# Spectral filter and gated feed-forward on one core: order of the inverse column transforms, number of half-blocks, places of folds, add-backs and loads

## The chip, the core and the metric

The kernel runs on one core of one Trainium2 chip. The metric is the device time of the whole program in microseconds (us). The median of three runs before the change is 499.27 us (499.16 to 499.53). TensorE multiplies matrices, VectorE (DVE) and ScalarE (ACT) work element by element and empty TensorE's accumulators (PSUM), GpSimd (POOL) does a few small operations, and SyncE (SP) issues nearly all DMAs.

## The reference

Two layers work on `x` of 2048 rows and 576 columns in bfloat16. The first is a global filter: layer norm, a real two-dimensional Fourier transform, a multiplication by a complex weight, the inverse transform, and the addition of `x`. The second is a feed-forward layer with a gate of width 4608.

```python
def _A_ref(x, w_r, w_i):
    X = rfft2(x.astype(float32), axes=(-2, -1))
    X = X * (w_r + 1j * w_i)
    return irfft2(X, s=(S, D), axes=(-2, -1)).astype(bfloat16)

def _B_ref(x, w_gate, w_up, w_down):
    return (gelu(x @ w_gate) * (x @ w_up)) @ w_down

h  = x + _A_ref(layernorm(x), w_r, w_i)
h2 = h + _B_ref(layernorm(h), w_gate, w_up, w_down)
```

## The kernel before, in words

All engines run instructions in the order in which the kernel's text issues them; that order is written out by hand. The 2048 rows lie as 16 tiles of 128 (`h_sb[:, h, :]`, `h` from 0 to 15). All transforms are matrix products on TensorE. PSUM is used as four rotating slots of two banks (`two`), so every use waits until the use four places before it has been emptied.

**Spectral part.** After the row transforms the work goes over nine "channels" `k` in the order 1, 2, ..., 7, 0 (0 carries 8 along). Per step of the loop at lines 668 to 706: `f2` and `f3` do forward products on TensorE, ScalarE copies their results, `wmul` on VectorE multiplies by the weights and writes a tile `Zt`, and `i3` does the inverse products of a channel from its `Zt` and the table `TI`. ScalarE (for one part VectorE) copies the results of `i3` into one of two collecting tiles: `EO[0]` takes channels 1 to 4, `EO[1]` takes 0 and 5 to 7. `inv_cols(x, g)` (line 632) then transforms the columns of pair `g` of row tiles (0 to 7) out of `EO[x]`: ten matmuls with weights of 58 rows into `cs_ps`, followed by an eviction with scaling into `cs` (pairs 0 and 1) or `cw`/`cwb` (pairs 2 to 7). `inv_cols(0, ...)` needs channels 1 to 4 alone; `inv_cols(1, ...)` needs all. Lines 707 to 715 set the order behind the loop: three transforms of `EO[0]`, channel 7's `i3`, four transforms, channel 0's `i3`, one transform. In the last step of the loop channel 6's `i3` stands ahead of all of them.

**Putting rows together.** `add_rows(g)` (line 757) multiplies pair `g` by the matrix `G16` into two PSUM slots `y_ps`, and the result is added to `h_sb`. For pairs 0 and 1 that is done at once. For pairs 2 to 7 it is spread over the feed-forward blocks in three steps: `fold` (line 745; four VectorE operations of 288 elements into `both`), `add_both` (line 780, the "add-back": eight matmuls and two VectorE additions), and `stats2` per row tile (line 785). After these, `norm2` (line 789) writes the normalised rows and `flip` (line 802) sends them by a transposing DMA, issued by SP, into `hl`, the matrix `Bt` read by the gate products. Row tiles 0 and 1 are transposed on TensorE instead; 2 and 3 go through `flip` during the first half-blocks.

**Feed-forward part.** Four chunks of 512 rows. For each chunk, 36 blocks of 128 gate and up columns (`gate`, line 889: 18 matmuls with 64-row weights, Gelu on ScalarE into `g_sb`, a multiplication on VectorE into `P_sb`, which frees the PSUM slot), then four down products (`acc`, line 938). Weights come in groups of three blocks (`load_gu`). The first chunk is split: `NH` half-blocks work on columns 0 to 255 (row tiles 0 and 1), before tiles 2 and 3 have arrived. The main loop then starts at its block 0; its blocks below `NH` work on columns 256 to 511 alone, and from block `NH` on they work on all 512.

`todo` is a table from the number of the block (0 to 143) to the small steps issued right behind that block; `after` is the same for the half-blocks. SP issues `flip`, `load_gu` and the loads of the down weights in the order of the text, and each of them waits at the head of SP's queue. `load_wd2` loads the last third of the down weights, `wd_2`, in six slices of two blocks each (288 KB); slice `i` holds blocks 24 + 2i and 25 + 2i.

Of the kernel before, what the change touches and what calls it, by code (L numbers as in the profile page):

```python
# [41 lines left out]
def kernel_body(  # L42
# [23 lines left out]
    def two(name):  # L66
        return psum.tile([P, 2, 512], FP32, name=name, tag="two", bufs=4)
# [72 lines left out]
    def load_gu(g, t=None):  # L140
        gc = slice(g % (NFT // FQ) * FQ * P, (g % (NFT // FQ) + 1) * FQ * P)
        if t is None:
            t = wgpool.tile([P, NR, FQ * P], BF16, name="wgu", tag="wgu")[:]
        for c, w in ((0, B_w_gate), (1, B_w_up)):
            nc.sync.dma_start(t[64 * c : 64 * c + 64], w[:, gc].rearrange("(r k) c -> k r c", k=64))
        return t
# [11 lines left out]
    NWA = 12  # L158
# [90 lines left out]
    def angle_c(sl):  # L249
        drop_sign(ab[:, sl], ab[:, sl])  # L250
# [4 lines left out]
    def cosine(sl):  # L255
        A.activation(TF[:, sl, 1, :], ab[:, sl], ACT.Sin, bias=nhpib[:], scale=2.0 * PI / S)

    def minus_sine(sl):
        V.tensor_scalar(TF[:, sl, 0, :], TF[:, sl, 2, :], -1.0, None, op0=ALU.mult)

    def turn_tf(sl):
        nc.sync.dma_start(
            TI[:, sl].rearrange("p k r q -> p (k r) q"), TF[:, sl].rearrange("p k r q -> p (k r q)"), transpose=True
        )
# [207 lines left out]
    def f2(c):  # L472
        ps = two("pq_ps")
        col = slice(slot[c] * P, (slot[c] + 1) * P)
        steps = [(par, t) for par in range(2) for t in (par, par + 2, 4)]
        if c == order[0]:
            steps.sort(key=lambda s: s[1] == 4)
        for par, t in steps:
            T.matmul(  # L479
                ps[:, par, 0:JP],  # L480
                lhsT=Bt[:, t, col],
                rhs=DT[:, t // 2, par] if t < 4 else DF[:, par],
                start=(t == par),
                stop=(t == 4),
            )
        pq[c] = wk.tile([P, 2, JP], BF16, name="pq", tag="pq", bufs=6)
        pq_ps[c] = ps

    def f2_out(c, copy=A.copy, rs=slice(0, 2)):
        copy(  # L490
            pq[c][:, rs].rearrange("p r (j a) -> p r j a", a=2),
            pq_ps[c][:, :, 0:JP].rearrange("p a (r j) -> p r j a", r=2)[:, rs],
        )
# [5 lines left out]
    def f3(k, half):  # L499
        ps = two("gh_ps")  # L500
        if k == 0:
            p0, p8 = pq[0], pq[8]
            t0, t1 = (NS, C) if half else (C, SN)
            for b, kk, p in ((0, 0, p0), (1, 8, p8)):
                comb(ps[:, b, 0:J], kk, t0, p[:, 0, 0:J], t1, p[:, 1, 0:J])
            if half == 0:
                xab[k] = wk.tile([P, 2, 2, JP], BF16, name="xab", tag="xab", bufs=2)
            A.copy(xab[k][:, half, :, 0:J], ps[:, :, 0:J])
            return
        p, q = pq[k], pq[k + 8]  # L510
        gh = wk.tile([P, 2, JP], BF16, name="hs" if half else "g", tag="hs" if half else "g", bufs=2)
        r = half
        comb(ps[:, r, 0:J], k, C, p[:, r, 0:J], SN, q[:, r, 0:J])
        comb(ps[:, 1 - r, 0:J], k, C, q[:, r, 0:J], NS, p[:, r, 0:J])
        if k == order[0] and half:
            hk[k] = ps
            return
        A.copy(gh[:, :, 0:J], ps[:, :, 0:J])
        if half == 0:
            gk[k] = gh  # L520
            return
        hk[k] = gh

    def sum_of(k, half):
        g, hs = gk[k], hk[k]
        if half == 0:
            xab[k] = wk.tile([P, 2, 2, JP], BF16, name="xab", tag="xab", bufs=2)
        x = xab[k]
        V.tensor_tensor(  # L529
            x[:, 1, ::-1, 0:J] if half else x[:, 0, :, 0:J],  # L530
            g[:, :, 0:J],
            hs[:, :, 0:J],
            ALU.add if half else ALU.subtract,
        )
# [97 lines left out]
    def inv_cols(x, g):  # L632

        ps = two("cs_ps")
        for w in range(NW):
            for e in range(2):
                rows = slice(64 * e, 64 * e + JW)
                T.matmul(  # L638
                    ps[:, e, 0:JP],
                    lhsT=EO[x][rows, w, 2 * g : 2 * g + 2].rearrange("p h e k l -> p (h e k l)"),  # L640
                    rhs=DQ[rows, w] if w or e else DT[rows, 0, :, 0, :],
                    start=(w == 0),
                    stop=(w == NW - 1),
                )
        pv = ps[:, :, 0:JP].rearrange("p t (q a) -> p t q a", q=2)
        if g >= 2:
            if x == 0 or g == 2:
                cw[x, g] = eop.tile([P, 2, JP], FP32, name=f"cw{x}{g}")[:]
            else:
                cw[x, g] = cwb[:, g - 3]  # L650
            dst = cw[x, g].rearrange("p t (a q) -> p t q a", q=2)
            if x == 0 and g == 6:
                V.tensor_scalar(dst, pv, Y_SCALE, None, op0=ALU.mult)
            else:
                A.activation(dst, pv, ACT.Copy, scale=Y_SCALE)
            return
        ts = eop.tile([P, 2, JP], BF16, name=f"cs{x}{g}")
        dst = ts[:].rearrange("p t (a q) -> p t q a", q=2)
        if x == 1 and g == 1:
            V.tensor_scalar(dst, pv, Y_SCALE, None, op0=ALU.mult)  # L660
        else:
            A.activation(dst, pv, ACT.Copy, scale=Y_SCALE)
        cs[x, g] = ts
# [4 lines left out]
    for i in range(n + 1):  # L668
        last = i >= n
        if not last:  # L670
            f2(order[i])
            if i != 1:
                f2_out(order[i])
        if i == 0:
            f2(order[0] + 8)
            angle_c(rest)
            cosine(rest)
            for r in range(2):
                f2_out(order[0] + 8, V.tensor_copy, slice(r, r + 1))
            minus_sine(rest)  # L680

        if 1 <= i <= n:
            f3(order[i - 1], 0)
            f3(order[i - 1], 1)
            if i == 1:
                f2_out(order[1])
                sum_of(order[0], 0)
                sum_of(order[0], 1)
            else:
                if i == 2:  # L690
                    turn_tf(rest)
                    pre = [load_gu(g) for g in range(3)]
                    nc.sync.dma_start(wd_a[:], wd_view[:, 0:NWA, :])
                wmul(order[i - 2], i - 1, order[i - 1])
        if not last and i:
            f2(order[i] + 8)
            f2_out(order[i] + 8)
        if i >= 3:
            for s in range(3):
                i3(order[i - 3], s)  # L700
        if last:
            wmul(order[i - 1], i)
        if i == 1:
            scr_pool.__exit__(None, None, None)
            eop = ctx.enter_context(tc.tile_pool(name="eop", bufs=1, side="right"))
            EO = [eop.tile([P, 5, H, 2, 4, 8], BF16, name=f"EO{x}", tag=f"EO{x}") for x in range(2)]
    for g in (0, 1, 2):
        inv_cols(0, g)
    for s in range(3):
        i3(order[6], s)  # L710
    for g in (3, 4, 5, 6):
        inv_cols(0, g)
    for s in range(3):
        i3(order[7], s)
# [157 lines left out]
    todo = {}  # L872
    for h in range(4, H):
        b = 6 * (h // 2 - 2)
        if h % 2 == 0:
            todo.setdefault((1, 6, 10, 13, 16, 19)[h // 2 - 2], []).append((fold, h // 2))
            todo.setdefault(b + 4, []).append((add_both, h // 2))
        todo.setdefault(b + 5 + h % 2, []).append((stats2, h))
        b = h // 4 * NFT - NFT + 3 * (h % 4) + 2 + 12 * (h < 8)
        todo.setdefault(b, []).append((norm2, h))  # L880
        todo.setdefault(b + 1, []).append((flip, h))

    for i in range(0, NWA, 2):
        todo.setdefault(16 + 3 * i // 2, []).append((load_wd2, slice(i, i + 2)))
    blk = 0
    groups = pre
    NG = NFT // FQ
# [15 lines left out]
        A.activation(g_sb, gu[:, 0, 0:n], ACT.Gelu_apprx_tanh)  # L903
        V.tensor_tensor(p_sb(f)[:, lo:hi], g_sb, gu[:, 1, 0:n], ALU.mult)  # L904

    NH = 11
    after = {
        0: [(sum_squares, 3), (norm2, 2), (flip, 2)],
        1: [(head_rstd, 3)],
# [1 line left out]
    }  # L911
    for f in range(NH):
        gate(0, f, groups[f // FQ], f % FQ, 0, 2 * P)
        for fn, h in after.get(f, ()):
            fn(h)
    for tcnk in range(4):
        for gi in range(NG):
            for i in range(FQ):
                f = gi * FQ + i
                gate(tcnk, f, groups[0], i, 2 * P if tcnk == 0 and f < NH else 0, 4 * P)  # L920
                for fn, h in todo.pop(blk, ()):
# [8 lines left out]
        for st in range(4):  # L930
            h = tcnk * 4 + st
# [85 lines left out]
```

## Time and profile before

| | |
|---|---|
| median of three runs | 499.27 us |
| profiled execution, whole | 499.36 us |
| its span | 497.6 us |
| TensorE busy | 487.6 us |
| VectorE busy | 224.5 us |
| ScalarE busy | 161.6 us |
| gate and up products, `gu` (line 895), share of the chain that ended last | 55% |
| down products, `acc` (line 938), share of that chain | 27% |
| column transforms, `cs_ps` (line 638), share of that chain | 2% |

The profile shows one execution, with all times from the start of its span. "PE" is TensorE's matmuls, "PEld" its weight loads, "SPq" SP's queue of DMA issues. A line of the time line has the start, the length, the engine, the line of the kernel, the operation, the tile written and those read, the shape, and the number merged; the idle time of the engine before it, with what ended it, stands in brackets. The chain lists start, length and work of what ended last. A table by stretches has, for each engine, the busy time and the number of instructions, then the granted clock, the busy share of the 16 DMA engines (over 1 where packets overlap) and GB/s. A matmul's shown length includes the time until its result is there, so starts of neighbours, not lengths, give the pace.

### The profile page before, as it was taken

To read this page: it belongs to the slowest core of one execution; us is meant where nothing else is said; L and a number is where in the kernel's file an instruction comes from. 1 tells how busy PE (TensorE), PEld (TensorE's weight loads), DVE (VectorE), ACT (ScalarE), POOL (GpSimd) and SP (SyncE) were. 2 spreads that over 40 slices of the span, in tenths; PEclk is the share of its full clock that TensorE was granted. 3 is DMA by queue.
4 is the path that set the end of the run, shared out by engine and by line. 5 is a ranking of instruction groups with operands and counts; after the bars stand their busy time and mean duration, and the time that the engine had idled before them with its cause. 6 is when DMAs were issued, how large, how long until landed. Compare 5 with 4: busy or idle time off the path is not lost.

```text
span 497.6 us, 12727 instructions
## 1 busy us (share of the span) xinstructions
PE 487.6 (98%) x5698; PEld 340.2 (68%) x5698; DVE 224.5 (45%) x442; ACT 161.6 (32%) x288; POOL 28.9 (6%) x78
## 2 busy tenths in 40 slices
PE   6999899999999999999999999999999999999997
PEld 2578689888879964444499844444799644445995
DVE  8999786988541244433311244333221333333111
ACT  8999873222211013233200132323110223233000
POOL 8500010201100000000000000000000000000000
PEclk9999999999999999999999999999999999999999
DMA  8739779959990019987730079987700287870000
GB/s 277 229 38 208 198 146 226 177 109 208 212 204 10 3 50 208 204 159 155 155 75 3 1 149 213 187 158 153 144 1 3 75 156 157 158 150 1 13 14 24
DMA packets 89549, 62.33 MB, mean 125 GB/s; under 512 B 23190, under 2 KB 88086, under 8 KB 89494
## 3 DMA queue, kind: packets, MB, share of 16 engines
q1 hardware_dynamic: 89206, 60.34, 60.9%
q0 software_dynamic: 288, 1.18, 0.8%
q8 instruction: 44, 0.72, 0.6%
q14 instruction: 11, 0.09, 0.1%
HBM read 52.65 MB, written 2.36 MB: 111 GB/s over the span
## 4 chain that ended last, share of the span: by engine, by line
PE 88%; DVE 7%; DMA 2%; SPq 1%; ACT 1%; issue 0%
PE gu L895 55%; PE acc L938 27%; PE cs_ps L638 2%; PE acc L957 2%; DVE m L547 2%; DMA h_sb<-in_A_x_dram 1%; PE y_ps L767 1%; SPq L421 1%; DVE xab L529 1%; DVE xn L136 1%; DVE st L117 1%; DVE st L116 1%; DVE Zt L567 0%; PE eo_ps L587 0%; ACT Bt L322 0%
## 5 line engine op out<-in xcount | busy, mean ns | idle before, releaser
L895 PE MATMUL gu<-Bt,wgu 64*128 64x512 bf16 (+1 forms) x2646 | 271.8, 363 | 0.0
L895 PEld LDWEIGHTS <-wgu 64*128 64x128 bf16 x2646 | 144.8, 94 | 123.6 <-DMA wgu<-in_B_w_up_dram 0.4
L904 DVE TENSOR_TENSOR P_sb<-g_sb,gu 128x512 bf16<-128x512 f32 (+1 forms) x155 | 99.9, 647 | 142.6 <-ACT g_sb L903 142.6
L903 ACT ACTIVATE g_sb<-gu 128x512 f32<-128x512 f32 (+1 forms) x155 | 87.8, 567 | 194.8 <-PE gu L895 194.0
L938 PEld LDWEIGHTS <-P_sb 64*128 64x128 bf16 x2160 | 132.7, 94 | 0.6
L938 PE MATMUL acc<-wd,P_sb 64*128 64x288 bf16 x1440 | 93.8, 283 | 0.0
L947 DVE TENSOR_TENSOR part<-part,acc 128x576 f32<-128x576 f32 x15 | 11.3, 754 | 111.3 <-ACT part L946 111.3
L938 PE MATMUL acc<-wd_a,P_sb 64*128 64x288 bf16 x720 | 49.7, 283 | 0.0
L946 ACT COPY part<-acc 128x576 f32<-128x576 f32 x15 | 9.6, 639 | 122.4 <-PE acc L938 122.4
L895 PE MATMUL gu<-Bt,wgu_e 64*128 64x256 bf16 (+1 forms) x144 | 12.5, 322 | 0.0
L792 DVE TENSOR_SCALAR hrow<-h_sb,mv,rstd 128x1152 bf16<-128x1152 bf16 x14 | 12.1, 868 | 0.6 <-POOL rstd L830 0.6
L479 PE MATMUL pq_ps<-DT,Bt 128*128 128x290 bf16 x64 | 12.3, 286 | 0.0
L949 DVE TENSOR_TENSOR h_sb<-h_sb,part 128x576 bf16<-128x576 bf16 x15 | 11.4, 758 | 0.5
L133 POOL TENSOR_TENSOR rstd<-rstd,mhalf 128x1 f32<-128x1 f32 (+1 forms) x16 | 11.4, 713 | 1.3
L895 PEld LDWEIGHTS <-wgu_e 64*128 64x128 bf16 x144 | 10.5, 94 | 1.3
L286 PE MATMUL f2t<-h_sb,ident 128*128 128x512 bf16 x27 | 7.8, 444 | 3.6 <-DMA h_sb<-in_A_x_dram 3.6
L479 PEld LDWEIGHTS <-Bt 128*128 128x128 bf16 x96 | 9.2, 97 | 2.5
L638 PE MATMUL cs_ps<-DQ,EO 58*128 58x290 bf16 x144 | 10.6, 283 | 0.0
L298 PE MATMUL f2t<-F,xn 128*128 128x256 bf16 x64 | 9.3, 275 | 1.4 <-DVE xn L136 1.4
L587 PE MATMUL eo_ps<-TI,Zt 128*128 128x256 bf16 x70 | 8.8, 273 | 1.3 <-DVE Zt L568 1.3
L490 ACT CAST pq<-pq_ps 128x580 bf16<-128x580 f32 x15 | 9.9, 663 | 0.2
L123 ACT ACTIVATE junk<-h_sb 128x576 bf16<-128x576 bf16 x14 | 9.4, 678 | 0.4 <-DMA h_sb<-in_A_x_dram 0.4
(138 smaller groups left out, 276.0 us busy)
## 6 DMA issues: line engine op xcount, KB each, us to landing
wgu<-in_B_w_gate_dram SPq DMA_DIRECT2D x46, 432.0 KB
wgu<-in_B_w_up_dram SPq DMA_DIRECT2D x46, 432.0 KB
wd_a<-in_B_w_down_dram SPq DMA_DIRECT2D x1, 1728.0 KB
wd<-in_B_w_down_dram SPq DMA_DIRECT2D x1, 1728.0 KB
wd<-in_B_w_down_dram SPq DMA_DIRECT2D x6, 288.0 KB
out_dram<-h_sb SPq DMA_DIRECT2D x3, 576.0 KB
h_sb<-in_A_x_dram SPq DMA_DIRECT2D x4, 288.0 KB
h_sb<-in_A_x_dram SPq DMA_DIRECT2D x2, 576.0 KB
```

What stands on the lines that cost most here:

```text
L133: G.tensor_tensor(dst[:, sl], dst[:, sl], mhalf[:, sl], ALU.pow)
L479: T.matmul(ps[:, par, 0:JP], lhsT=Bt[:, t, col], rhs=DT[:, t // 2, par] if t < 4 else DF[:, par], start=(t == par), stop=(t == 4),)
L547: V.tensor_tensor(m[:, :, :, js], x[:, :, :, js], w[:, sl, js].unsqueeze(1).to_broadcast([P, 2, 2, n]), ALU.mult)
L638: T.matmul(ps[:, e, 0:JP], lhsT=EO[x][rows, w, 2 * g : 2 * g + 2].rearrange("p h e k l -> p (h e k l)"), rhs=DQ[rows, w] if w or e else DT ...
L792: V.tensor_scalar(hrow[:], h_sb[:, h, :].rearrange("p (r k) -> p r k", k=64).unsqueeze(2).to_broadcast([P, NR, 2, 64]), mv2[:, h, 0:1], rs ...
L895: T.matmul(gu[:, c, 0:n], lhsT=w[rows, r, i * P : (i + 1) * P], rhs=hl[tcnk % 2][rows, r, lo:hi], start=(r == 0), stop=(r == NR - 1),)
L903: A.activation(g_sb, gu[:, 0, 0:n], ACT.Gelu_apprx_tanh)
L904: V.tensor_tensor(p_sb(f)[:, lo:hi], g_sb, gu[:, 1, 0:n], ALU.mult)
L938: T.matmul(accs[i][:, c, 0:DH], lhsT=p_sb(f)[rows, st * P : (st + 1) * P], rhs=wd[f // NWA][rows, f % NWA, c * DH : (c + 1) * DH], start=( ...
L947: V.tensor_tensor(part, part, accs[1][:, :, 0:DH], ALU.add)
L949: V.tensor_tensor(hv, hv, part, ALU.add)
L957: T.matmul(acc[:, 0, 0:DH], lhsT=p_sb(f)[:, st * P : (st + 1) * P], rhs=wd[f // NWA][:, f % NWA, cc], start=(f == 0), stop=(f == NFT - 1),)
```

## The change

Four edits, in program order. First, `inv_cols(0, 0)` and `inv_cols(0, 1)` are issued inside the last step of the loop ahead of channel 6's `i3`. Behind the loop there are then three transforms (2, 3, 4), channel 7's `i3`, two (5, 6), channel 0's `i3`, and the last one, as before. Second, `NH` is 10 instead of 11. Third, the folds move from behind blocks 1, 6, 10, 13, 16, 19 to 4, 8, 11, 14, 17, 20; the add-backs from 4, 10, 16, 22, 28, 34 to 6, 12, 18, 24, 30, 36; the statistics go two blocks later with them. `norm2` and `flip` keep their places. Fourth, the six slices of `wd_2` are issued behind blocks 17, 21, 25, 29, 33, 35 instead of 16, 19, 22, 25, 28, 31.

```diff
         if not last and i:
             f2(order[i] + 8)
             f2_out(order[i] + 8)
+        if last:
+            inv_cols(0, 0)
+            inv_cols(0, 1)
         if i >= 3:
             for s in range(3):
                 i3(order[i - 3], s)
...
-    for g in (0, 1, 2):
+    for g in (2, 3, 4):
         inv_cols(0, g)
     for s in range(3):
         i3(order[6], s)
-    for g in (3, 4, 5, 6):
+    for g in (5, 6):
         inv_cols(0, g)
     for s in range(3):
         i3(order[7], s)
...
     for h in range(4, H):
         b = 6 * (h // 2 - 2)
         if h % 2 == 0:
-            todo.setdefault((1, 6, 10, 13, 16, 19)[h // 2 - 2], []).append((fold, h // 2))
-            todo.setdefault(b + 4, []).append((add_both, h // 2))
-        todo.setdefault(b + 5 + h % 2, []).append((stats2, h))
+            todo.setdefault((4, 8, 11, 14, 17, 20)[h // 2 - 2], []).append((fold, h // 2))
+            todo.setdefault(b + 6, []).append((add_both, h // 2))
+        todo.setdefault(b + 7 + h % 2, []).append((stats2, h))
...
-    for i in range(0, NWA, 2):
-        todo.setdefault(16 + 3 * i // 2, []).append((load_wd2, slice(i, i + 2)))
+    for i, bk in enumerate((17, 21, 25, 29, 33, 35)):
+        todo.setdefault(bk, []).append((load_wd2, slice(2 * i, 2 * i + 2)))
...
-    NH = 11
+    NH = 10
```

## The prediction

> **What bounds the kernel now.** I read the busy shares first, then the chain that ended last, then TensorE's waits, then the time line around each place that the edits touch.
>
> ```profile
> PE 487.6 (98%) x5698; PEld 340.2 (68%) x5698; DVE 224.5 (45%) x442; ACT 161.6 (32%) x288; POOL 28.9 (6%) x78
> PE 88%; DVE 7%; DMA 2%; SPq 1%; ACT 1%; issue 0%
> ...
> 69.47 15.73 PE gu L895 x288
> ...
> 104.89 11.66 PE gu L895 x108
> ```
>
> TensorE is 98% busy, so only its gaps and its overheads can be won. The two chain rows give the prices of its work: 288 matmuls are 16 half-blocks, 0.983 us each; 108 are 6 full blocks, 1.943 us each. The waits show few gaps behind the first 51 us:
>
> ```profile
> PE eo_ps L587 <- DVE Zt L568: 1.3, 1, 1.3
> PE y_ps L767 <- DVE P_sb L904: 0.2, 1, 0.2
> ```
>
> The time line of TensorE shows where they lie (start, length, what; in brackets the idle time):
>
> ```profile
> 50.43 0.29 PE L497 MATMUL gh_ps<-pq,TF 128*128 128x289 bf16 x1
> 51.98 1.27 PE L587 MATMUL eo_ps<-TI,Zt 128*128 128x256 bf16 x10 [1.26 <-DVE Zt L568]
> 53.17 0.29 PE L638 MATMUL cs_ps<-DT,EO 58*128 58x290 bf16 x1
> ...
> 58.95 1.31 PE L611 MATMUL eo_ps<-TI,Zt 128*64 128x128 bf16 x40
> ...
> 80.01 1.36 PE L895 MATMUL gu<-Bt,wgu 64*128 64x256 bf16 x21
> ...
> 91.77 0.98 PE L767 MATMUL y_ps<-both,G 64*128 64x288 bf16 x8 [0.19 <-DVE P_sb L904]
> 92.48 1.24 PE L895 MATMUL gu<-Bt,wgu_e 64*128 64x512 bf16 x9
> ```
>
> At 51.98 channel 6's products wait for its `Zt`, which VectorE finishes at 51.92; VectorE has no gap from 31 us on, so nothing brings that time forward. 80.01 is block 0 of the main loop, the first work on columns 256 to 511, and it did not wait. The last two rows are the second add-back, late.
>
> **Step 1, the transforms ahead of channel 6.** One column transform takes 0.62 us (53.17, 53.81, 54.43 start its neighbours); two take 1.24. The last matmul before the gap starts at 50.43 and needs 289 columns at the rate of the stream, 0.12 us, so TensorE is free at about 50.55. The trace shows 0.09 us more at each change between full-height and 64-row matmuls (start to start 0.21 us at 52.97 to 53.17, against 0.11 within a run). The two transforms then run 50.64 to 51.88, and with the change back TensorE is ready at 51.97: the gap is filled to the last tenth, and channel 6 still starts at 51.98. Behind it the sequence is three transforms, channel 7, two, channel 0. Channel 7 starts at 55.15 as before (its `Zt` is written at 55.08). Channel 0 started at 58.95 and now starts 1.24 earlier, 57.71; its `Zt`, last written by the operation at 56.90 for 0.46, is there at 57.36. Cover for the added evictions: ScalarE idled 1.14 us from 51.92 (its row at 53.06), and two evictions at 0.67 each end at 53.26, so channel 6's copy slips 0.2. Four rotating PSUM slots carry all of this. The tightest reuse is the third moved-up transform, at 54.46 in the slot of channel 6's copy, free at about 54.3: 0.13 us to spare. Everything behind follows TensorE in relative time. **-1.24 us**; bounds -1.24 and 0 (if slots come free late).
>
> **Step 2, ten half-blocks instead of eleven.** Two halves become one full block: 2 x 0.983 - 1.943 = **-0.02**. But the main loop now begins one half-block sooner after the work before it: 80.01 - 0.98 = 79.03 on the old time line. Its first weights wait for the flips of rows 2 and 3 (DMA transposes issued by SP). The share and GB/s of the DMA engines, last two columns, show them:
>
> ```profile
> 73.04 1.33 SPq L804 DMA_TRANSPOSE Bt<-hrow  x1
> 75.23 1.62 SPq L804 DMA_TRANSPOSE Bt<-hrow  x1
> 74.00:75.50 1.50, 1.50 (x32) 1.38 (x28) 1.23 (x4) 0.48 (x2) 0.29 (x1) 1.00 1.92 171
> 75.50:77.00 1.50, 1.50 (x32) 1.38 (x30) 0.94 (x4) 0.67 (x2) 0.00 (x0) 1.00 0.37 7
> 77.70:78.50 0.80, 0.80 (x20) 0.73 (x18) 0.42 (x1) 0.20 (x2) 0.00 (x0) 1.00 1.57 24
> 78.50:79.10 0.60, 0.60 (x16) 0.56 (x12) 0.33 (x1) 0.23 (x1) 0.00 (x0) 1.00 1.13 253
> 104.00:105.57 1.57, 1.57 (x21) 1.40 (x19) 0.50 (x1) 0.60 (x1) 0.00 (x0) 1.00 1.05 199
> ```
>
> They move bytes until 79.10, with two stretches of almost none; the completion increments of the second come at 79.63 to 79.78. Before, that was 0.23 us early; now it is 0.75 late. The flips' own start hangs on TensorE's earlier work by way of VectorE and POOL, so the 1.24 shifts both alike. **+0.75 us**; bounds 0 and +1.0.
>
> The fourth flip, alone, moved its bytes in 1.57 us (last row) and completed 3.3 us after its issue at 102.81. At that pace the second one would be there at 75.23 + 3.3 = 78.5, before 79.03, and the term would be 0.
>
> The Trainium skill ("DMA: Bandwidth & Descriptors", "Latency and other measured facts") gives DMA transposes 261 GB/s, and its section "Anatomy of one DMA" a fixed cost of about 2.0 us for a DMA issued by GpSimd. My estimate from that page is 2.0 + 295 KB / 261 GB/s = 3.1 us, so no wait here, and a sum lower by 0.75. The lone flip agrees; these two took 5.8 and 4.6 us, and the measurement decides.
>
> **Step 3, folds and add-backs.** Removed: the stall at 91.77. Half-block 10 freed TensorE at 91.41, the eight add-back matmuls take 0.48 undisturbed, and the next block began at 92.48: 0.58 us lost, because fold 3 and two sets of statistics held up the VectorE operations (0.33 each) that free PSUM. **-0.58**. The new schedule puts add-back 2 two half-blocks behind its fold, where three lay between. VectorE's rows after block 1, placed after block 4 (B = end of its matmuls):
>
> ```profile
> 82.70 0.42 DVE L904 TENSOR_TENSOR P_sb<-g_sb,gu 128x256 bf16<-128x256 f32 x1 [0.56 <-ACT g_sb L903]
> 83.03 0.45 DVE L753 TENSOR_TENSOR both<-cw 128x288 bf16<-128x288 f32 x1
> ...
> 84.14 0.45 DVE L754 TENSOR_TENSOR both<-cw 128x288 bf16<-128x288 f32 x1
> 84.51 0.42 DVE L904 TENSOR_TENSOR P_sb<-g_sb,gu 128x256 bf16<-128x256 f32 x1
> ```
>
> Block 1 ended at 80.01 + 2 x 0.983 = 81.98, so the fold's last output is ready at B + 2.16 + 0.45 + 0.05 = 2.66. The add-back's last pair wants it at B + 1.97 + 0.36 = 2.33: +0.33. Half-block 7 then wants the slot of half-block 5, freed at B + 2.53 + 0.41 + 0.05 = 2.99, where TensorE is ready at 2.78: +0.21. Add-back 3, at block 12, has fold 3 (block 8) long behind it. At block 17 row 5's normalisation (0.79) and fold 6 (1.48) lie in front of block 18's multiply: its slot is free at B + 0.93 + 0.60 + 0.79 + 1.48 + 0.69 + 0.05 = 4.54, block 20 wants it at 2 x 1.943 + 0.48 = 4.37: +0.16. The other folds have blocks of 1.943 with 0.61 of VectorE work in them. **+0.70**; bounds 0 and +1.0. Add-back 7 goes to block 36, behind the down products; their slots are emptied under block 36, and nothing waits.
>
> **Step 4, the loads of `wd_2`.** On SP's queue five of six move behind flips and weight loads; the last two go behind the load for group 13. Between 112 and 144 us the DMA engines run without a break at about 210 GB/s, first come first served. The load for group 11, issued at 125.88, came at 137.0 and cost 0.10 us; with one slice (295 KB, 1.4 us) less ahead of it that goes: **-0.10**. The last slices trade places with the load that completed at 148.5, so they come by 148.5; the first down product starts at 143.12, takes 8.82, and reads them from 143.12 + 8.82 x 32/36 = 150.96. 2.5 us to spare: 0.
>
> **Sum.** -1.24 - 0.02 + 0.75 - 0.58 + 0.70 - 0.10 = -0.49. The profiled execution took 499.36 (span 497.6 and 1.76 around it), 0.09 above the median of 499.27. 499.36 - 0.49 = 498.87, as a median 498.8.
>
> **Rivals.** *The flips come in time* (30%). For it: the lone flip's row; the stall between 75.5 and 77.0 has no cause in the edit, and may not recur. Against: the same two flips, the same instructions around them. Sum without the 0.75: 498.0, faster.
> *The last `wd_2` slices are late* (7%): the down product waits at 150.96 for a load issued only after block 33. It turns the sign when the lateness eats the 2.5 us, the 0.5 gained and 1.0 more, so at 4 us later than first come first served makes them, about 152.5; then 500.3 or more. Against: the DMA engines' rate falls to 143 GB/s in 144 to 152, so the queue is running empty there.
> *The transforms do not fill the gap* (5%): their slots or evictions come late, step 1 is worth 0, and the rest adds up to +0.75: 500.0 as a median, within 0.2%.
>
> **How the numbers follow.** A run of this kernel can tell about 0.2%, 1.0 us, from no change. The main case holds 53%: 498.8, own range 498.3 to 499.5. Faster by over 1.0 us: the flips' case and the lower edge of the main one, 0.34. Slower: the late slices and 5% for a VectorE backlog that I have not seen, 0.12. Range 497.8 to 500.0: it holds the flips' case with 0.2 below it and leaves out the late slices.
>
> **What the new profile would show.** Two `cs_ps` transforms at 50.6 and channel 6 still at 52.0; channel 0 at 57.7; a wait of 0.7 us before block 0, near 77.8, for DMA; waits of 0.5 us together in and behind add-back 2, near 85.5; none in add-back 3. Wrong it would be with channel 6 later than 52.1, no wait at block 0, or a wait inside the first down product.

## The result, and the profile after

The changed kernel takes 498.29 us as the median of 16 runs (498.12 to 498.68), against 499.25 us for the kernel before, also 16 runs: a ratio of 0.9981, 95% interval 0.9973 to 0.9988. That is 0.96 us less, just inside the 0.2% that the prediction called no change, and inside its range. The interval leaves 1 out: with 16 runs of each kernel it is about 0.4 us wide to either side, so the gain is small but clear.

The profiled execution of the changed kernel is the slowest of its 16: 498.68 us, span 496.9. So it shows the places of the gain better than its size. The page's first line of busy times, and the one entry of TensorE's list of waits that was not in the one before and lies behind the first 26 us:

```profile
PE 488.5 (98%) x5678; PEld 331.1 (67%) x5680; DVE 224.7 (45%) x441; ACT 161.3 (32%) x287; POOL 29.1 (6%) x78
```

```profile
PE gu L898 <- DMA Bt<-hrow: 0.5, 1, 0.5
```

The waits for channel 6's `Zt` (1.3 us) and at an add-back (0.2 us) have left the list. A wait for the flips has come in. The time line of TensorE at the same places as before:

```profile
50.64 0.29 PE L497 MATMUL gh_ps<-pq,TF 128*128 128x289 bf16 x1
50.86 0.29 PE L638 MATMUL cs_ps<-DT,EO 58*128 58x290 bf16 x1
...
52.22 1.27 PE L587 MATMUL eo_ps<-TI,Zt 128*128 128x256 bf16 x10
...
55.39 1.26 PE L587 MATMUL eo_ps<-TI,Zt 128*128 128x256 bf16 x10
...
57.94 1.31 PE L611 MATMUL eo_ps<-TI,Zt 128*64 128x128 bf16 x40
...
78.83 0.92 PE L898 MATMUL gu<-Bt,wgu 64*128 64x256 bf16 x13 [0.54 <-DMA Bt<-hrow]
...
85.70 0.91 PE L770 MATMUL y_ps<-both,G 64*128 64x288 bf16 x8
86.65 1.05 PE L898 MATMUL gu<-Bt,wgu 64*128 64x256 bf16 x16
...
95.42 0.67 PE L770 MATMUL y_ps<-both,G 64*128 64x288 bf16 x8
95.92 1.46 PE L898 MATMUL gu<-Bt,wgu_e 64*128 64x512 bf16 x11
```

Two transforms stand from 50.86 in what was the gap. Channel 0 starts at 57.94 instead of 58.95. That is 1.0 and not 1.24 us, because this execution was already 0.21 us late when the last forward product began (50.64 against 50.43), ahead of every edit. For the same reason channel 6 starts at 52.22, later than the 52.1 that the prediction named as a sign of being wrong. Counted from the last forward product it starts after 1.58 us, where the prediction had 51.98 - 50.43 = 1.55. In the trace with nine half-blocks (below), which has the same order of transforms and in which that product starts at 50.42, channel 6 starts at 52.00. Block 0 waits for the flips and starts at 78.83. The brackets count idle time only behind the end of a matmul's shown length; by starts the loss is larger. The last half-block's final matmul starts at 78.02, so in the undisturbed stream block 0 would follow at 78.03: 0.80 us lost. The first add-back and what follows take 86.65 - 85.70 = 0.95 us where 0.49 is undisturbed: 0.46 lost. The second one is undisturbed again (95.92 - 95.42 = 0.50).

The chain that ended last shows the new wait in its place. It now runs through the second flip, between VectorE's and TensorE's work:

```profile
73.32 0.87 DVE hrow L795
74.19 0.03 DVE P_sb L907
74.22 4.47 DMA Bt<-hrow
78.69 0.14 issue
78.83 5.10 PE gu L898 x90
```

From here on "lost" is always this distance between the start that came and the start of an undisturbed stream. By the same measure the second add-back of the kernel before lost 0.68 us (92.48 - 91.31 - 0.49, with 91.31 the end of two half-blocks that start at 89.35), not the 0.58 that I had read. The expectations below still have 0.70 us for the wait at block 0, 0.44 for the one at the first add-back and 0.58 for this one; by this measure they are 0.80, 0.46 and 0.68.

### The profile page after: what moved, and what is told of

It reads as the page before. It is cut to its first block, busy times and chain, and to the rows that moved or that the text cites. A ratio compares the mean times of both kernels' runs of the same rounds, so it can differ in the third digit from the quotient of the medians.

```text
span 496.9 us, 12686 instructions
## 1 busy us (share of the span) xinstructions
PE 488.5 (98%) x5678; PEld 331.1 (67%) x5680; DVE 224.7 (45%) x441; ACT 161.3 (32%) x287; POOL 29.1 (6%) x78
## 4 chain that ended last, share of the span: by engine, by line
PE 93%; DVE 2%; ACT 2%; DMA 1%; POOL 1%; issue 0%; POOLq 0%; ACTq 0%
PE gu L898 54%; PE acc L941 27%; PE pq_ps L479 2%; PE cs_ps L638 2%; PE acc L960 2%; PE eo_ps L587 2%; PE f2t L286 1%; PE y_ps L770 1%; DMA Bt<-hrow 1%; PE gh_ps L497 1%; PE gh_ps L496 1%; ACT Bt L322 1%; DMA h_sb<-in_A_x_dram 1%; ACT junk L123 1%; DVE hrow L795 0%
## 5 line engine op out<-in xcount | busy, mean ns | idle before, releaser
L898 PEld LDWEIGHTS <-wgu 64*128 64x128 bf16 x2646 | 148.3, 94 | 119.7 <-issue 1.2
L941 PEld LDWEIGHTS <-P_sb 64*128 64x128 bf16 x2160 | 122.2, 94 | 10.9
L941 PE MATMUL acc<-wd,P_sb 64*128 64x288 bf16 x1440 | 90.9, 283 | 0.0
L941 PE MATMUL acc<-wd_a,P_sb 64*128 64x288 bf16 x720 | 46.8, 283 | 0.0
L286 PE MATMUL f2t<-h_sb,ident 128*128 128x512 bf16 x26 | 9.0, 505 | 3.8 <-DMA h_sb<-in_A_x_dram 3.7
L898 PE MATMUL gu<-Bt,wgu_e 64*128 64x512 bf16 (+1 forms) x126 | 12.3, 345 | 0.0
L132 POOL TENSOR_SCALAR rstd<-mv 128x1 f32<-128x1 f32 (+1 forms) x16 | 4.1, 256 | 104.2 <-DVE mv L118 103.9
L898 PEld LDWEIGHTS <-wgu_e 64*128 64x128 bf16 x126 | 7.1, 94 | 4.3
```

What stands on the lines that cost most here:

```text
L286: T.matmul(dst, lhsT=ident[:], rhs=h_sb[:, 0, 0:512], start=True, stop=True)
L898: T.matmul(gu[:, c, 0:n], lhsT=w[rows, r, i * P : (i + 1) * P], rhs=hl[tcnk % 2][rows, r, lo:hi], start=(r == 0), stop=(r == NR - 1),)
L941: T.matmul(accs[i][:, c, 0:DH], lhsT=p_sb(f)[rows, st * P : (st + 1) * P], rhs=wd[f // NWA][rows, f % NWA, c * DH : (c + 1) * DH], start=( ...
```

## The experiments

Each was timed beside the kernel before on the same chip. There were four chips, and the kernel before had medians of 499.33, 499.34, 499.39 and 499.43 us on them, against 499.25 beside the changed kernel. So a difference of 0.1 to 0.2 us between two medians from different chips tells nothing.

### Each edit alone

**The order of the transforms.**

```diff
+        if last:
+            inv_cols(0, 0)
+            inv_cols(0, 1)
...
-    for g in (0, 1, 2):
+    for g in (2, 3, 4):
...
-    for g in (3, 4, 5, 6):
+    for g in (5, 6):
```

> Only the new order of the column transforms; half-blocks, folds and loads as before. Theory (the two transforms fill the wait for channel 6's Zt): 1.24 us less than before, 498.0; channel 0 starts 1.24 us earlier, and the waits of 0.58 us at the second add-back and of 0.1 us at the weights of block 33 stay. Rival (PSUM slots or evictions come late and eat the gain): 499.0 to 499.3.

Measured: 498.12 us against 499.33, ratio 0.9975 (0.9965 to 0.9985). Channel 0 lies 7.30 us behind the last forward product (50.84 to 58.14) where it lay 8.52 before. The second add-back still waits. Time line of TensorE in this run:

```profile
50.84 0.29 PE L497 MATMUL gh_ps<-pq,TF 128*128 128x289 bf16 x1
51.06 0.29 PE L638 MATMUL cs_ps<-DT,EO 58*128 58x290 bf16 x1
...
58.14 1.31 PE L611 MATMUL eo_ps<-TI,Zt 128*64 128x128 bf16 x40
...
90.96 0.98 PE L770 MATMUL y_ps<-both,G 64*128 64x288 bf16 x8 [0.19 <-DVE P_sb L907]
```

The theory holds: 1.2 us. This edit alone does at least as well as all four together: its median is lower, but the intervals of the two ratios overlap.

**Ten half-blocks.**

```diff
-    NH = 11
+    NH = 10
```

> Only ten half-blocks instead of eleven. Theory (block 0 then waits 0.70 us for the flips, and the wait of 0.58 us at the second add-back goes because block 10 is a full one): 0.70 - 0.58 - 0.02 = +0.10, 499.35. Rival one (the wait for the flips in the changed kernel has another cause, and is not there with the old order): 498.65. Rival two (the second add-back waits all the same): 499.95.

Measured: 499.01 us against 499.33, ratio 0.9993 (0.9984 to 1.0002). Time line of TensorE:

```profile
79.72 2.03 PE L895 MATMUL gu<-Bt,wgu 64*128 64x256 bf16 x34 [0.31 <-DMA Bt<-hrow]
...
91.97 0.67 PE L767 MATMUL y_ps<-both,G 64*128 64x288 bf16 x8
92.47 0.83 PE L895 MATMUL gu<-Bt,wgu_e 64*128 64x512 bf16 x6
```

Both places are as the theory has them: the wait for the flips is there with the old order too, so rival one falls; and the second add-back runs undisturbed, so rival two falls. Only the size was off. Block 0 loses 0.57 us here, not 0.80, and 0.57 - 0.68 - 0.02 = -0.13. The median says -0.3, and the interval takes in both.

**Later folds, add-backs and statistics.**

```diff
-            todo.setdefault((1, 6, 10, 13, 16, 19)[h // 2 - 2], []).append((fold, h // 2))
-            todo.setdefault(b + 4, []).append((add_both, h // 2))
-        todo.setdefault(b + 5 + h % 2, []).append((stats2, h))
+            todo.setdefault((4, 8, 11, 14, 17, 20)[h // 2 - 2], []).append((fold, h // 2))
+            todo.setdefault(b + 6, []).append((add_both, h // 2))
+        todo.setdefault(b + 7 + h % 2, []).append((stats2, h))
```

> Only the later folds, add-backs and statistics. Theory (the stall of 0.58 us at the second add-back is traded for 0.44 at the first and 0.05 at block 20, as the changed kernel's trace has them): -0.09, 499.15. Rival (the first add-back waits in the changed kernel only because of the shorter run of half-blocks before it): -0.58, 498.67.

Measured: 499.19 us against 499.33, ratio 0.9996 (0.9987 to 1.0005). The first add-back waits with eleven half-blocks as it does with ten:

```profile
87.15 1.00 PE L767 MATMUL y_ps<-both,G 64*128 64x288 bf16 x8
88.18 0.61 PE L895 MATMUL gu<-Bt,wgu 64*128 64x256 bf16 x8
```

From 87.15 to 88.18 it is 1.03 us where 0.49 is undisturbed: 0.54 lost. The rival falls: one wait is traded for another of nearly the same size. The interval of the times holds the theory's -0.09 and no change alike, and it is the trace that decides here.

**Later loads of `wd_2`.**

```diff
-    for i in range(0, NWA, 2):
-        todo.setdefault(16 + 3 * i // 2, []).append((load_wd2, slice(i, i + 2)))
+    for i, bk in enumerate((17, 21, 25, 29, 33, 35)):
+        todo.setdefault(bk, []).append((load_wd2, slice(2 * i, 2 * i + 2)))
```

> Only the later loads of wd_2. Theory (one slice less ahead of the weights of block 33 takes away their wait of 0.1 us, and the last slices still come in time): -0.1, 499.15, no wait in the first down product. Rival (the last slices come late): over 499.25, with a wait inside the first down product.

Measured: 499.26 us against 499.33, ratio 0.9998 (0.9989 to 1.0007): nothing. The first down product has no wait, so the rival falls. But the theory's gain can't be claimed either. The wait of 0.1 us at block 33 that it was to remove stands in the profiled execution of the kernel before and in none of the traces of the transforms' order, the ten half-blocks or the folds alone, all of which keep the old loads. It was in one execution of the four that have the old loads, so these runs can't tell whether the edit removes it.

### The size of each wait

**Eleven half-blocks in the changed kernel, and nine.**

```diff
-    NH = 10
+    NH = 11
```

> The changed kernel with eleven half-blocks again. Theory (the wait of 0.70 us at block 0 is for the flips, and eleven half-blocks cover it): 0.68 us less than the changed kernel's 498.29, 497.6. Rival (the wait is made up elsewhere, or moves to another place): 498.3.

```diff
-    NH = 10
+    NH = 9
```

> The changed kernel with nine half-blocks. Theory: block 0 asks for the flips another 0.98 us sooner and waits 0.70 + 0.98 = 1.68 us; less 0.02 for one block fewer: 499.25. Rival (the length of the wait does not hang on the number of half-blocks): 498.3.

Measured: 497.75 us with eleven and 499.25 us with nine, where ten takes 498.29. The waits for the flips, eleven (none listed; the row is block 0's start) and then nine:

```profile
78.81 2.89 PE L898 MATMUL gu<-Bt,wgu 64*128 64x256 bf16 x49
```

```profile
78.28 3.45 PE L898 MATMUL gu<-Bt,wgu 64*128 64x256 bf16 x60 [1.19 <-DMA Bt<-hrow]
```

By these medians one half-block fewer cost 0.96 us, as the step of 0.98 - 0.02 has it, and one more gave back 0.54. By the differences to the kernel before on the same chip (-0.09 with nine, -0.96 with ten, -1.59 with eleven) it is 0.87 and 0.63. In the seven traces with ten half-blocks block 0 loses 0.47 to 0.57 us in four and 0.71 to 0.80 in three. So the wait at ten is 0.5 to 0.6 us in the middle, and one half-block less adds nearly a half-block's length to it. The rivals fall.

**The first fold earlier.**

```diff
-            todo.setdefault((4, 8, 11, 14, 17, 20)[h // 2 - 2], []).append((fold, h // 2))
+            todo.setdefault((2, 8, 11, 14, 17, 20)[h // 2 - 2], []).append((fold, h // 2))
```

> The changed kernel with the first fold behind block 2 instead of block 4. Theory (the 0.44 us of waits in and behind the first add-back come from a fold that ends too late before it): they go, 497.85. Rival (VectorE's load in these half-blocks sets them, wherever the fold stands): 498.3.

Measured: 498.00 us, ratio to before 0.9976 (0.9966 to 0.9986), and runs from 497.71 to 498.86. In its trace the first add-back runs undisturbed (85.20 to 85.69, 0.49 us). The theory holds for the place; the gain by medians is 0.3, with the flips' wait of 0.52 us still there.

**One transform ahead of channel 6.**

```diff
         if last:
             inv_cols(0, 0)
-            inv_cols(0, 1)
...
-    for g in (2, 3, 4):
+    for g in (1, 2, 3, 4):
```

> The changed kernel with one column transform ahead of channel 6 instead of two, and four behind it. Theory (each transform moved into the gap saves its own 0.62 us): 0.62 us more than the changed kernel, 498.9, with 0.6 us of the wait for channel 6's Zt back. Rival (the gain comes from the new grouping behind channel 6): 498.3.

Measured: 498.92 us. TensorE's list of waits has the old one back, at less than half its length:

```profile
PE eo_ps L587 <- DVE Zt L568: 0.5, 1, 0.5
```

The median is 0.63 us higher for one transform out of the gap. The traces agree: channel 0 lies 8.52 us behind the last forward product with no transform in the gap, 7.89 (50.49 to 58.38) with one and 7.30 with two. The gain is the filling of the gap, transform by transform.

### What makes the flips late

In all fourteen traces the second flip is issued 6.01 to 6.03 us after the first half-block starts, and completes between 10.14 and 10.57 us after it. Block 0 asks for it at 9.82 with ten half-blocks and 10.80 with eleven. In all of them the DMA engines also have the two stretches in which they move almost nothing.

**Later load behind the flips, and a later second flip.**

```diff
-        2: [(norm2, 3), (flip, 3), (load_wd, 1)],
+        2: [(norm2, 3), (flip, 3)],
+        6: [(load_wd, 1)],
```

> The changed kernel with the load of the second third of the down weights (1728 KB) issued by SP behind half-block 6 instead of half-block 2, where it follows the second flip at once. Theory (the stretch of 0.7 us in which the second flip moves almost nothing comes from the DMA issued right behind it): the second flip completes about 9.5 us after the first half-block starts instead of 10.2 to 10.5, before block 0 asks for it at 9.8; the wait of 0.4 to 0.7 us goes, 497.9. Rival (the stretch belongs to the transposing DMA or to an instruction fetch): completion at 10.2, 498.3.

```diff
-        2: [(norm2, 3), (flip, 3), (load_wd, 1)],
+        2: [(norm2, 3)],
+        3: [(flip, 3)],
+        6: [(load_wd, 1)],
```

> As the run with the late load of down weights, and the second of the two flips issued one half-block later (0.98 us). Theory (the first flip stops for 1.1 us while SP issues the second one, about 6.3 to 7.4 us after the first half-block starts): the first flip completes at about 8.1 or its stop moves with the issue to 7.3, and the second completes 3.3 us after its issue, at 10.3; 0.5 us of wait at block 0, 498.3. Rival (the stop is tied to an instruction fetch near 5.7): the first flip stops at 6.3 as before and completes at 9.2.

Measured: 498.30 and 498.38 us. Neither tells anything of its theory, because neither edit moved an issue. SP's queue of the first of them:

```profile
71.83 3.49 SPq L807 DMA_TRANSPOSE Bt<-hrow  x2
75.37 0.58 SPq L729 DMA_DIRECT2D wd<-in_B_w_down_dram  x1
```

The load still follows the flips at once. SP runs its own queue, and where nothing in it waits for TensorE, a later place in the text is the same place on SP. The two runs are repeats of the changed kernel, and agree with it within 0.1 us.

**The load behind one that does wait.**

```diff
-        2: [(norm2, 3), (flip, 3), (load_wd, 1)],
+        2: [(norm2, 3), (flip, 3)],
...
+    todo.setdefault(3, []).append((load_wd, 1))
     blk = 0
     groups = pre
```

> The changed kernel with the 1728 KB load of down weights placed behind main block 3, so that on SP's queue it follows the load of a weight group, which waits for TensorE; no DMA is then issued behind the two flips for about 6 us. Theory (the second flip's stop of 0.7 us comes from the DMA issued right behind it): the second flip completes about 9.5 us after the first half-block starts instead of 10.2, the wait of 0.4 us at block 0 goes, 497.9. Rival (the stop belongs to the transposing DMA itself or to an instruction fetch): completion at 10.2, 498.3, or up to 0.2 less if the big load only competes for the DMA engines at its end.

Measured: 498.23 us, ratio 0.9976 (0.9966 to 0.9985), the same as the changed kernel. Now SP's queue is free behind the flips:

```profile
72.03 3.95 SPq L807 DMA_TRANSPOSE Bt<-hrow  x2
81.93 0.60 SPq L145 DMA_DIRECT2D wgu<-in_B_w_gate_dram  x1
82.58 0.63 SPq L145 DMA_DIRECT2D wgu<-in_B_w_up_dram  x1
83.27 0.62 SPq L729 DMA_DIRECT2D wd<-in_B_w_down_dram  x1
```

The stretches of almost no transfer stay (last columns of the table by stretches: share of the DMA engines, GB/s):

```profile
73.23:74.70 1.47, 1.47 (x32) 1.35 (x28) 1.39 (x3) 0.69 (x2) 0.04 (x1) 1.00 1.13 205
74.70:75.25 0.55, 0.55 (x14) 0.50 (x12) 0.53 (x2) 0.07 (x1) 0.00 (x0) 1.00 0.89 19
75.25:76.10 0.85, 0.85 (x20) 0.78 (x18) 0.31 (x1) 0.38 (x1) 0.00 (x0) 1.00 1.25 18
...
76.60:77.30 0.70, 0.70 (x18) 0.64 (x14) 0.42 (x1) 0.14 (x1) 0.00 (x0) 1.00 1.85 18
77.30:78.10 0.80, 0.80 (x18) 0.64 (x13) 0.35 (x1) 0.38 (x1) 0.00 (x0) 1.00 0.97 210
```

The second flip completes 10.45 us after the first half-block. My theory falls: the load behind it is not what stops it. What does is open. The first stretch begins in each trace about 0.3 to 0.5 us into SP's issue of the second flip, and in thirteen of fourteen it ends 0.2 to 0.3 us after that issue does (with a short burst in between in two of them). In the trace with one transform ahead the issue lasts until 8.76 us after the first half-block, and bytes move again from 7.2 to 7.7. An instruction fetch also lies near the stretch in each trace; no run here moved the one without the other.

### A version that beats both

```diff
-    NH = 10
+    NH = 11
...
-            todo.setdefault((4, 8, 11, 14, 17, 20)[h // 2 - 2], []).append((fold, h // 2))
+            todo.setdefault((2, 8, 11, 14, 17, 20)[h // 2 - 2], []).append((fold, h // 2))
```

> The changed kernel with eleven half-blocks and the first fold behind block 2. Theory (the two waits are separate, and each edit takes its own away): 498.29 - 0.4 - 0.44 = 497.4, no wait over 0.1 us in the main loop. Rival (one of the waits turns up at another add-back): 497.75.

Measured: 497.34 us in five runs (one of them at 498.2), ratio to the kernel before 0.9964 (0.9950 to 0.9978), 0.95 us under the changed kernel and as much under its repeat with the late load (498.30), which ran on the same chip. TensorE's whole list of waits is then:

```profile
PE f2t L286 <- DMA h_sb<-in_A_x_dram: 3.7, 1, 3.7
PE f2t L298 <- DVE xn L136: 0.6, 1, 0.6
PE pq_ps L479 <- DVE Bt L328: 0.2, 1, 0.2
```

All of it lies in the first 26 us. The two waits that the change had brought were separate, and each edit takes its own away.

## Why the prediction was right

It forecast 498.8 us and no measurable change. The time came at 498.29, in its range of 497.8 to 500.0, and 0.96 us under before is still within its 1.0, but only just. The gain is twice the forecast 0.49, and 498.29 lies just outside the 498.3 to 499.5 that the prediction gave its main case, between that case and the rival in which the flips come in time (498.0). The time alone would not tell these two apart; the wait at block 0 in every trace with ten half-blocks does. The places of the gain and of the waits were foreseen, while half of the gain was not. Point by point:

- **Step 1 was right, in place and size.** Forecast -1.24; the edit alone gave 498.12 - 499.33 = -1.21, one transform less cost 0.63. Filling the gap "to the last tenth" is how it came out: channel 6 follows the second transform with only the usual 0.21 us between starts.
- **Step 2 had the right mechanism and too large a size.** The wait at block 0 is there and answers to the number of half-blocks. Forecast +0.75; the changed kernel's profile shows 0.80, but its runs usually 0.5 (0.54 by eleven half-blocks, and 0.47 to 0.57 in the four traces with ten where the second flip's issue took 1.3 us). I took the flip's completion from one execution, 10.57 us after the first half-block, which is the latest of the fourteen traces; in most it is near 10.2. I also put nothing for the time from the completion to the first matmul, which is 0.13 to 0.14 us in the seven traces with ten half-blocks (78.69 to 78.83 in the chain above). The two errors go against each other: 10.2 - 9.82 + 0.14 = 0.52 in most executions, and 10.49 - 9.82 + 0.14 = 0.81 in the changed kernel's profile, which came near 0.75 by luck.
- **Step 3 was right in kind, with three terms mis-sized.** The removed stall was 0.68 and not 0.58; the new waits at the first add-back 0.46 and not 0.54; at block 20 0.05 and not 0.16. As forecast it is nearly an exchange: -0.68 + 0.51 = -0.17, forecast +0.12, the edit alone -0.14, within its noise.
- **Step 4 failed as a gain and held as a risk.** The -0.10 was a wait in one execution of four with the old loads. The last slices came in time, as argued.
- **The sum.** With these sizes it is -1.24 - 0.02 + 0.50 - 0.68 + 0.46 + 0.05 = -0.93, and the measured difference is -0.96. The forecast of -0.49 missed by the flips (0.25) and the add-backs (0.29), less the loads (0.10).
- **The rivals.** The flips did not come in time: the wait was there in every trace with ten half-blocks. The 3.3 us of the lone flip (the third that SP issues, for row tile 4), and the estimate of 3.1 us from the Trainium skill's page "DMA: Bandwidth & Descriptors", were not reached by a second of two flips in any trace: 4.1 to 4.6 us. No slices of `wd_2` came late, and the transforms did fill the gap.

The edits do not add up one by one. Ten half-blocks and the later folds each remove the same stall at the second add-back, so together they remove it once and pay for two new waits. The four single gains (1.21, 0.32, 0.14 and 0.07) add up to 1.74; with the stall of 0.68 counted once it is 1.06, near the measured 0.96. The prediction put this stall down to the folds alone, which did not change its sum. By the traces' sizes the other three edits together cost 0.3 us, and so the reorder alone (498.12) is at least as good as the whole change.

## What to carry to other kernels

Moving independent work into a wait was worth its own length here (0.6 us for one transform, 1.2 for two, in a wait that held two), with its buffers free in time; that could be read from the time line beforehand. Taking away filler work (here a half-block) was worth next to nothing by itself on a busy engine (0.02 us), and exposed what it covered: look up when the covered transfer completes, in more than one execution if there is one. Where a time of completion decides the sign of a term, its spread between executions belongs in the range.

## What was not expected of the hardware

- Two transposing DMAs issued 2.2 us apart by SP took 5.3 to 5.8 us (the first) and 4.1 to 4.6 us (the second) from issue to completion, in all fourteen traces. The third flip, issued with no other flip near it and when the DMA engines moved little or nothing, took 3.2 to 3.3 us in all of them. It is the only one of that kind: the eleven later flips, each issued by itself while weight loads were under way, took 4.8 to 8.5 us. So 3.3 us is the time with idle DMA engines, not that of any flip issued by itself. The DMA engines move under 25 GB/s for 1.0 to 1.6 us in the middle of the first flip and for 0.7 to 0.9 us in the second. Keeping the next large load away for 6 us did not change it.
- The second flip's completion, counted from TensorE's first half-block, varied by 0.43 us between executions, although its issue began within 0.02 us of the same time. The late ones (10.37 and more) are those in which the issue itself took 1.4 us or more instead of 1.3. In these the first flip completes late as well, after 9.4 to 9.6 us instead of 9.2 to 9.3.
